# Letting a list scheduler choose VectorE or GpSimd, and DMA or TensorE, in an attention stage that runs beside a dense expert layer

## The chip, the cores and the metric

One core of a Trainium2 chip. The metric is the device time of one execution, in microseconds (us). Engine names are those of the profile: PE (TensorE matmul), PEld (its weight loads), DVE (VectorE), ACT (ScalarE), POOL (GpSimd), SP (SyncE, the queue from which the DMAs are issued).

## What is computed

Three layers follow one another; q, k and v have shape (4, 8, 576, 64).

```python
scores = scale * np.matmul(q, k.transpose(0, 1, 3, 2))     # plus a decay, causal mask
attn = np.exp(scores - max); attn = attn / (np.sum(attn) + 1e-09)
x = np.matmul(attn, v)                                      # (2304, 512)
for e in range(4):                                          # dense expert layer
    out += p[:, e:e + 1] * (np.maximum(x @ w1[e], 0.0) @ w2[e])
logits = out @ phi                                          # soft mixture: 8 experts x 4 slots
d = softmax over tokens; slot_out = experts(d.T @ out); y = softmax over slots @ slot_out
```

## The kernel before

Values are kept as two fp16 parts, a high part (the rounded value) and a low part (what rounding left), and each product is taken as high*high + high*low + low*high, so nearly every operand is made in two steps: high (ACT or POOL), then low (DVE).

**Attention.** A unit is 128 query rows of one batch with its 8 heads (18 units); a group is 1, 2 or 4 heads of a unit (76 groups). A group goes through: scores on PE (`g_scores`, L1077, two PSUM buffers `s`), row maximum on DVE (`g_max`, L1098), its product with the scale of q on POOL (`g_bias`, L1105), exp on ACT (`g_exp`, L1118), which frees the `s` buffer, the high part of the probabilities on POOL (`g_hi`, L943 by the helper `scaled`), the low part on DVE (`g_lo`, L1135), a transposition of both parts (`transposed`; by DMA at L854, or for the first groups on PE at L868 with copies out of PSUM at L873 and L875), and the product with v (`g_pv`, L1166). Two buffers hold probabilities, three hold high and low parts, five hold transposed ones. The finished unit is normalized (`fin_a`), split (`fin_h` on POOL, `fin_l` on DVE L1196) and transposed. q, k and v are scaled, split (low parts at L1018, L956, L979) and q and k transposed in the same way.

**Expert 0 beside it.** The first expert of the dense layer (`e0_l1` L526, `e0_l2` L547) takes a unit as soon as it is transposed, and fills PE between the groups. Experts 1 to 3 follow (L711 and L587): for blocks of rows their first layer is done as a fast matrix multiplication with 7 products of halves instead of 8, for which sums of x parts (`x_sums`, L631) and of weight blocks (`part` with `sub`, L475, low parts L481) are made on DVE. The last stage is the soft mixture.

**What sets the order.** `Sched` is a list scheduler that runs when the program is built. Every piece of work is a task with an engine, a cost in us, a key (its priority), the tasks it needs, and a condition on buffers. Whenever an engine is free in the scheduler's own account, the ready task of lowest key is emitted to it. On the chip each engine then runs its instructions in that order, whatever the real times. In the kernel before, only high parts of q, k, v and weights may go to either of two engines (`HI`), and every transposition has a fixed way: PE for the first few (`PE_P`, `PE_X`, `PE_Q`, `PE_K`), DMA for all others.

Of the kernel before, what the change touches and what calls it, by code (L numbers as in the profile page):

```python
# [30 lines left out]
W_COST = {"Act": 0.62, "DVE": 0.65}  # L31
X_COST = {"Act": 0.74, "DVE": 0.88}
# [6 lines left out]
PE_K = (0, 1, 2)  # L39
K_W1, K_W2, K_PB = -6, 1, 2.0  # L40
# [94 lines left out]
class Sched:  # L135
# [4 lines left out]
    DMA_HEAD, DMA_TAIL = 1.4, 1.6  # L140

# [46 lines left out]
    def run(self, done):  # L188
        while not done():
            started = False  # L190
            for e in self.engines:
# [3 lines left out]
                for x in self.ready[e]:  # L195
                    if (best is None or x.key < best.key) and (x.can is None or x.can()):
                        best = x
# [7 lines left out]
                if e == "DMA":  # L205
                    end = max(self.t + self.DMA_HEAD, self.free[e] + self.DMA_HEAD) + best.dur
                    self.free[e] = end - self.DMA_HEAD
                    end += self.DMA_TAIL
                else:
                    end = self.t + best.dur  # L210
                    self.free[e] = end
# [21 lines left out]
def moe_attention_kernel(ctx: ExitStack, tc: tile.TileContext, q, k, v, f, probs, w1, w2, phi, s1, s2, out):  # L233
# [145 lines left out]
    later = sc.later  # L379

# [34 lines left out]
    def w_steps(e, ti, pages):  # L415
# [50 lines left out]
        def lo(g):  # L466
            nc.vector.scalar_tensor_tensor(
                out=lo_[:, g * per:(g + 1) * per, :], in0=raw[g], scalar=am[:, 7:8],
                in1=hi_[:, g * per:(g + 1) * per, :], op0=ALU.mult, op1=ALU.subtract)
        def part(c, ps):  # L470
# [3 lines left out]
            def sub(out, a, b):  # L474
                return lambda: nc.vector.tensor_tensor(out=out, in0=a, in1=b, op=ALU.subtract)  # L475
# [4 lines left out]
            def lo_of(b, o):  # L480
# [6 lines left out]
                    ("DVE", sub(b11, b12, b11), (1,)), ("Act", hi_of(b22, 2), ()), ("DVE", lo_of(b21, 1), (2,)),  # L487
                    ("Act", hi_of(b11, 4), (3,)), ("DVE", lo_of(b22, 2), (4,)), ("DVE", sub(b12, b22, b12), (3,)),
                    ("DVE", sub(b22, b22, b11), (7, 8)), ("DVE", sub(b21, b21, b22), (5, 9)),
# [10 lines left out]
        X = [(lambda eng="Act", g=g: hi(g, eng), lambda g=g: lo(g)) for g in range(4)]  # L500
# [114 lines left out]
    def x_sums(p, tmp):  # L615
# [14 lines left out]
        def op(o, x, y, f, *deps):  # L630
            return ("DVE", lambda: nc.vector.tensor_tensor(out=at_(o), in0=at_(x), in1=at_(y), op=f), deps)  # L631
# [32 lines left out]
    def steps(key, todo, cost, deps):  # L664

        out = []
        for eng, fn, ds in todo:
            out.append(sc.task(eng, cost[eng], key, fn, [out[d] for d in ds] if ds else deps))
        return out

    def halves_tasks(e, w1_t, w2_t, s_t, tmps, between=lambda j: [], used_up=None):
# [24 lines left out]
        def quad(p, m, h_t):  # L696
# [26 lines left out]
            def add(o, x, n, deps, last=True):  # L723
# [4 lines left out]
                return T("DVE", 0.47, -30, go, deps)  # L728

            def split(i, c, y, t):  # L730
                h_, l_ = (z[:, y] for z in hT2[i])
                t = T("Act", 0.41, -30, lambda: nc.scalar.activation(out=h_, in_=tmp[:, c], func=AF.Relu), [t])  # L732
                t = T("DVE", 0.47, -30, lambda: nc.vector.scalar_tensor_tensor(  # L733
# [9 lines left out]
            t0 = T("Act", 0.37, -30, copy, [mul(1, a11, 0)] + mem[m % 2])  # L743
# [13 lines left out]
        def tile_l2(j, t, hs):  # L757
# [15 lines left out]
            return T("DVE", 0.66, -30, out, [y])  # L773
# [75 lines left out]
    def transposed(key, deps, dst, src, r, nw, done, can, way):  # L849

        m = r.stop - r.start
        if way == "DMA":
            def go():
                nc.sync.dma_start_transpose(out=dst(), in_=src())  # L854
                if done:
                    later(done)
            return sc.join([sc.task("DMA", 0.112 * nw * m / 128 + 0.38, key, go, deps, can)])
        cell, left, copies = {}, [], []
        t = None
        for w0 in range(0, nw, 8):  # L860
# [1165 lines left out]
```

## Time and profile before

| | |
|---|---|
| median of 3 runs | 1016.6 us (1015.73 to 1016.62) |
| the profiled execution | 1015.85 us, span in the trace 1014.1 us |
| PE busy | 924.8 us (91%) |
| DVE busy | 685.6 us (68%) |
| ACT busy | 384.3 us (38%) |
| POOL busy | 173.4 us (17%) |
| mean granted clock of PE | 0.972 |

Busy shares are means over stages with different limits: attention with expert 0 runs to about 390 us, experts 1 to 3 to about 950 us, the soft mixture to the end. The trace shows one execution; the sum of the prediction is made against its 1015.85 us, of which 1.75 us lie outside the span.

### The profile page before, as it was taken

The page shows a single profiled execution, that of the slowest core. Times are in us where ns is not written, and L with a number is a line of the kernel's source. Part 1 is how long each engine was busy: PE and PEld are TensorE (multiplying, and loading weights), DVE is VectorE, ACT ScalarE, POOL GpSimd, SP SyncE. Part 2 cuts the span into 40 slices and gives each one's busy share as a digit, 9 for nine tenths or more (in the row PEclk, how much of TensorE's full clock was granted, in tenths as well). Part 3 has the DMA queues.
Part 4 walks back from the last instruction along what each step waited for, and adds up shares of the span by engine and source line. Part 5 has one row for each costly group of instructions (what it writes and reads, how often), then busy time and mean ns, then how long its engine had stood idle before and what let it go on. Part 6 is the DMA issues. An engine that isn't in the chain of part 4 may idle for free.

```text
span 1014.1 us, 20126 instructions
## 1 busy us (share of the span) xinstructions
PE 924.8 (91%) x8165; PEld 568.3 (56%) x8165; DVE 685.6 (68%) x1408; ACT 384.3 (38%) x843; POOL 173.4 (17%) x227
## 2 busy tenths in 40 slices
PE   4478888989988998999999999999999999999994
PEld 3467676777776765446454554545455465555431
DVE  7998998896897789979467692816765283323313
ACT  7656555555654347335024440302422031112122
POOL 1755645464353300000000000000000000000000
PEclk9597999999999999999999999999999999999998
DMA  9468999999999822013201331000113028222695
GB/s 268 105 151 180 191 188 192 194 189 200 199 183 205 152 65 81 22 42 126 83 1 42 118 130 43 1 1 1 45 52 125 1 72 290 98 67 84 210 358 187
DMA packets 274413, 125.29 MB, mean 124 GB/s; under 512 B 246384, under 2 KB 246384, under 8 KB 274320
## 3 DMA queue, kind: packets, MB, share of 16 engines
q1 hardware_dynamic: 274272, 123.93, 49.5%
q8 instruction: 64, 1.05, 0.4%
q14 instruction: 29, 0.24, 0.1%
q10 hardware_dynamic: 48, 0.07, 0.0%
HBM read 73.58 MB, written 4.72 MB: 77 GB/s over the span
## 4 chain that ended last, share of the span: by engine, by line
PE 56%; DVE 7%; issue 2%; ACT 2%; DMA 1%; POOL 1%; DVEq 0%; ACTq 0%; POOLq 0%
PE pso L587 27%; PE q L711 18%; PE psh L569 3%; DVE arena L725 2%; DVE arena L631 2%; PE fh L1920 1%; PE fo L1937 1%; DVE arena L733 1%; DMA arena<-arena 1%; PE psh L526 1%; PE lg L1709 1%; PE sl L1734 1%; PE pt L1699 1%; DVE arena L481 1%; DVE arena L1135 1%
## 5 line engine op out<-in xcount | busy, mean ns | idle before, releaser
L587 PE MATMUL pso<-arena 128*128 128x512 f16 x1296 | 284.8, 379 | 1.0 <-DVE arena L733 0.9
L711 PE MATMUL q<-arena 128*128 128x384 f16 x1344 | 221.9, 326 | 2.3 <-DVE arena L725 1.4
L587 PEld LDWEIGHTS <-arena 128*128 128x128 f16 x1296 | 125.8, 98 | 153.2 <-issue 4.1
L711 PEld LDWEIGHTS <-arena 128*128 128x128 f16 x1344 | 131.2, 98 | 90.9 <-issue 3.6
L1118 ACT ACTIVATE arena<-s,mx,qs 128x320 f32<-128x320 f32 (+4 forms) x144 | 91.8, 646 | 120.4 <-POOL mx L1105 119.7
L725 DVE TENSOR_TENSOR arena<-arena,q 128x384 f32<-128x384 f32 x224 | 117.0, 548 | 18.4 <-PE q L711 16.2
L593 DVE SCALAR_TENSOR_TENSOR arena<-pso,pw,arena 128x512 f32<-128x512 f32 x54 | 40.4, 749 | 122.9 <-PE pso L587 122.8
L732 ACT ACTIVATE arena<-arena 128x384 f16<-128x384 f32 x128 | 65.8, 521 | 121.8 <-DVE arena L725 121.6
L526 PE MATMUL psh<-arena 128*128 128x128 f16 x1728 | 106.5, 224 | 4.4 <-DMA arena<-arena 1.8
L526 PEld LDWEIGHTS <-arena 128*128 128x128 f16 x1728 | 102.0, 101 | 5.3 <-issue 2.7
L547 PE MATMUL pso<-arena 128*128 128x512 f16 x432 | 99.5, 380 | 1.5 <-ACT arena L536 0.8
L1077 PE MATMUL s<-arena 128*128 128x128 f16 (+1 forms) x928 | 69.8, 219 | 31.0 <-ACT arena L1118 26.9
L1135 DVE SCALAR_TENSOR_TENSOR arena<-arena 128x512 f16<-128x512 f32 (+4 forms) x148 | 77.9, 566 | 20.2 <-POOL arena L943 20.2
L1077 PEld LDWEIGHTS <-arena 128*128 128x128 f16 x928 | 61.5, 102 | 35.7 <-issue 31.4
L733 DVE SCALAR_TENSOR_TENSOR arena<-arena 128x384 f16<-128x384 f32 x128 | 69.5, 553 | 14.3 <-ACT arena L732 9.3
L943 POOL TENSOR_SCALAR arena<-arena 128x576 f16<-128x576 f32 (+4 forms) x76 | 64.6, 850 | 56.4 <-ACT arena L1118 26.1
L1098 DVE TENSOR_REDUCE mx<-s 128x1 f32<-128x576 f32 (+4 forms) x76 | 63.6, 845 | 3.6 <-PE s L1077 3.6
L547 PEld LDWEIGHTS <-arena 128*128 128x128 f16 x432 | 40.1, 98 | 46.2 <-DVE arena L538 1.7
L1601 POOL TENSOR_SCALAR_AFFINE_SELECT arena<-arena 128x32 f32<-128x32 f32 x3 | 0.6, 216 | 379.5 <-PE q L711 379.4
L1166 PE MATMUL pv<-arena 128*128 128x64 f16 (+1 forms) x1312 | 51.7, 196 | 12.3 <-DMA arena<-arena 8.1
L1105 POOL TENSOR_SCALAR mx<-mx,qs 128x2 f32<-128x2 f32 (+2 forms) x76 | 43.8, 576 | 90.1 <-DVE mx L1098 73.6
L1166 PEld LDWEIGHTS <-arena 128*128 128x128 f16 (+1 forms) x1312 | 46.1, 101 | 19.8 <-DMA arena<-arena 10.7
(204 smaller groups left out, 966.0 us busy)
## 6 DMA issues: line engine op xcount, KB each, us to landing
arena<-in_moe_w_dram SPq DMA_DIRECT2D x58, 512.0 KB, 4.1
arena<-in_moe_w_dram SPq DMA_DIRECT2D x69, 256.0 KB, 5.1
arena<-in_moe_w_dram SPq DMA_DIRECT2D x9, 768.0 KB, 8.7
arena<-in_k_dram SPq DMA_DIRECT2D x16, 256.0 KB, 3.6
arena<-in_q_dram SPq DMA_DIRECT2D x16, 256.0 KB, 3.7
arena<-in_v_dram SPq DMA_DIRECT2D x16, 256.0 KB, 3.9
out_dram<-arena SPq DMA_DIRECT2D x16, 256.0 KB, 2.7
arena<-in_moe_w_dram SPq DMA_DIRECT2D x3, 1024.0 KB, 6.1
```

The lines of the kernel that those rows point to most:

```text
L526: nc.tensor.matmul(out=ps[:, m, :], lhsT=wt["w1" + a, 0][:, kk, ms], rhs=xT[j][:, b + kk, ts], start=(n == 0), stop=(n == 3 * KD - 1))
L547: nc.tensor.matmul(out=ops[u], lhsT=a[:, m, ts], rhs=wt["w2" + b, 0][:, m, :], start=(m == 0 and z == 0), stop=(m == KF - 1 and z == 2))
L587: nc.tensor.matmul(out=ps, lhsT=a[:, m, ts], rhs=wt["w2" + b, e][:, m, :], start=(m == 0 and z == 0), stop=(m == KF - 1 and z == 2))
L711: nc.tensor.matmul(out=ps[n], lhsT=wS[e][o][:, y, k, ms], rhs=x[z][:, k], start=(i == 0), stop=(i == 5))
L725: nc.vector.tensor_tensor(out=tmp[:, o], in0=tmp[:, x], in1=ps[n], op=ALU.add)
L732: t = T("Act", 0.41, -30, lambda: nc.scalar.activation(out=h_, in_=tmp[:, c], func=AF.Relu), [t])
L733: t = T("DVE", 0.47, -30, lambda: nc.vector.scalar_tensor_tensor(out=l_, in0=tmp[:, c], scalar=0.0, in1=h_, op0=ALU.max, op1=ALU.subtract) ...
L943: nc.gpsimd.tensor_scalar(out=out, in0=x, scalar1=scale, scalar2=0.0, op0=ALU.mult, op1=ALU.add)
L1077: nc.tensor.matmul(out=o, lhsT=qT[u][:, 2 * h + w, :], rhs=kT[kk][:, 2 * h + w, k0:k0 + n_], start=(w == 0), stop=(w == 1 and mask is None))
L1118: nc.scalar.activation(out=P[:, x], in_=sv[:, x // hb, x % hb], func=AF.Exp, scale=qs[u][:, 4:5], bias=mxs[n][:, 4 + x:5 + x], accum_out=s ...
L1135: nc.vector.scalar_tensor_tensor(out=t[:, :, d0:d0 + n_], in0=P[:, :, s0:s0 + n_], scalar=P_MUL, in1=t[:, :, s0:s0 + n_], op0=ALU.mult, op ...
L1166: nc.tensor.matmul(out=pv[u][r, h, :], lhsT=pt[:, w, r], rhs=rhs, start=(z == 0), stop=(z == len(mm) - 1))
```

## The change

- The scheduler gets costs per engine, and a rule (`soonest`): a task that may go to two engines is left for the other one if that one, with what is queued there ahead, would be done over `SLACK` sooner.
- Low parts of probabilities, q, k, v, x and expert 0's weights, and the sums for experts 1 to 3 (`x_sums`, `sub`) may go to DVE or POOL. On POOL a low part with a scale takes two instructions (scale in place, then subtract).
- exp adds ln 4096 to its bias, so its result is already scaled; the high part of the probabilities then may go to POOL or ACT, and the low part is a plain subtraction. The division by the sum takes the factor out again.
- `g_bias` moves from POOL to ACT.
- Every transposition after the first few goes to DMA, or to PE if the DMA queue is more than `T_WAIT` behind in the scheduler's account and a PSUM buffer is there; on PE it is 8 windows at a time, with a copy by DVE or ACT.
- The scheduler's costs are changed nearly everywhere, most of them upwards.

```diff
+T_WAIT = 1.0
+    def soonest(self, x, e):
+        for o in x.eng:
+            if o != e:
+                before = sum(y.dur[o] for y in self.ready[o] if y.key < x.key and len(y.eng) == 1)
+                if max(self.free[o], self.t) + before + x.dur[o] + self.SLACK < self.t + x.dur[e]:
+                    return False
+        return True
...
+    LO = ("DVE", "Pool")
+    def low(eng, out, x, scale, hi_):
+        if eng == "DVE":
+            nc.vector.scalar_tensor_tensor(out=out, in0=x, scalar=scale, in1=hi_, op0=ALU.mult, op1=ALU.subtract)
+        else:
+            nc.gpsimd.tensor_scalar(out=x, in0=x, scalar1=scale, scalar2=0.0, op0=ALU.mult, op1=ALU.add)
+            nc.gpsimd.tensor_tensor(out=out, in0=x, in1=hi_, op=ALU.subtract)
...
+        def rule(x, e):
+            return e == "DMA" or (m_can() and sc.free["DMA"] > sc.t + T_WAIT)
+        engs = ("DMA", "PE") if way == "any" else (way,)
+        sc.task(engs, {"DMA": 0.17 * nw * m / 128 + 0.05, "PE": pe_t(chunks[0][1] * m)}, key, go, deps,
+                can if way != "PE" else lambda: m_can() and (can is None or can()), rule if way == "any" else None)
...
-        nc.gpsimd.tensor_scalar(out=mx[:, 4:4 + nh], in0=mx[:, 0:nh], scalar1=qs[u][:, 4:5], scalar2=None,
-                                op0=ALU.mult)
+        nc.scalar.activation(out=mx[:, 4:4 + nh], in_=mx[:, 0:nh], func=AF.Copy, scale=qs[u][:, 4:5],
+                             bias=math.log(P_MUL))
...
-            nc.vector.scalar_tensor_tensor(out=t[:, :, d0:d0 + n_], in0=P[:, :, s0:s0 + n_], scalar=P_MUL,
-                                           in1=t[:, :, s0:s0 + n_], op0=ALU.mult, op1=ALU.subtract)
+            by[eng].tensor_tensor(out=t[:, :, d0:d0 + n_], in0=P[:, :, s0:s0 + n_], in1=t[:, :, s0:s0 + n_],
+                                  op=ALU.subtract)
...
-                t = T(P_HI, 0.1 + nh * nco * 1.0e-3, n + 0.3, lambda eng, n=n: g_hi(n, eng), [t_exp[n]], lambda: hl_r.free)
-                t = T("DVE", 0.14 + nh * nco / 960, n + 0.4, lambda n=n: g_lo(n), [t])
+                t = T(HI, hi_t(nh * nco), n + 0.3, lambda eng, n=n: g_hi(n, eng), [t_exp[n]], lambda: hl_r.free)
+                t = T(LO, lo_t(nh * nco, 1 + (i > 0)), n + 0.4, lambda eng, n=n: g_lo(n, eng), [t])
...
-                                "PE" if n < PE_P else "DMA")]
+                                "PE" if n < PE_P else "any")]
```

What the scheduler makes of it, counted over the whole program: 76 biases go from POOL to ACT; of the 148 low parts of probabilities 78 go to POOL (26,496 of 51,200 columns) and 70 stay on DVE; of the 66 low parts of q, k, v and expert 0's weights 28 go to POOL; 6 of 18 `fin_l`, 22 of 42 sums for x and 23 of 24 for weights go to POOL. ACT takes 45 high parts of probabilities and x that POOL had. 23 DMA transpositions go to PE (262 of 1,352 windows of 128 columns, and 16 of 64), whose transposing matmuls rise from 224 to 502, and their copies on DVE from 10 to 34, on ACT from 10 to 27.

Three places show it. First, SP's queue, from its first half-height transposition of k on (`128x16x64`); L854 and L920 are the transpositions, L988 and L1037 loads of q. Before:

```order
L854 DMA_TRANSPOSE arena<-arena 128x16x64
L988 DMA arena<-in_q_dram 128x8x64
L854 DMA_TRANSPOSE arena<-arena 128x9x128
L854 DMA_TRANSPOSE arena<-arena 128x16x128
L854 DMA_TRANSPOSE arena<-arena 128x9x128
L854 DMA_TRANSPOSE arena<-arena 128x16x128
L854 DMA_TRANSPOSE arena<-arena 128x9x128 x2
L854 DMA_TRANSPOSE arena<-arena 128x16x128 x2
L988 DMA arena<-in_q_dram 128x8x64
L854 DMA_TRANSPOSE arena<-arena 128x8x128 x2
```

Now:

```order
L920 DMA_TRANSPOSE arena<-arena 128x16x64
L1037 DMA arena<-in_q_dram 128x8x64
L920 DMA_TRANSPOSE arena<-arena 128x9x128 x2
L920 DMA_TRANSPOSE arena<-arena 128x16x128 x2
L920 DMA_TRANSPOSE arena<-arena 128x9x128
L1037 DMA arena<-in_q_dram 128x8x64
L920 DMA_TRANSPOSE arena<-arena 128x16x128 x2
L1037 DMA arena<-in_q_dram 128x8x64
L920 DMA_TRANSPOSE arena<-arena 128x8x128
```

One of four 9-window transpositions and one of two 8-window ones are gone from the queue and are done on PE, and the loads of q stand earlier.

Second, ACT in the unit whose groups are 2 heads of 448 columns; L1118 and L1166 are exp, L1153 the new bias, L992 high parts, L588 and L554 an eviction of expert 0. Before:

```order
L1118 ACTIVATE arena,sums<-s,mx,qs 128x448 x2
L554 ACTIVATE arena<-pso,pw 128x512
L1118 ACTIVATE arena,sums<-s,mx,qs 128x448 x4
L995 ACTIVATE arena,qs<-arena 128x512
L904 ACTIVATE arena,kvs<-arena 128x512
L875 ACTIVATE arena<-tp 128x8x128
L1118 ACTIVATE arena,sums<-s,mx,qs 128x448 x2
```

Now:

```order
L1153 ACTIVATE mx<-mx,qs 128x2
L1166 ACTIVATE arena,sums<-s,mx,qs 128x448 x2
L1153 ACTIVATE mx<-mx,qs 128x2
L1166 ACTIVATE arena,sums<-s,mx,qs 128x448 x2
L588 ACTIVATE arena<-pso,pw 128x512
L992 ACTIVATE arena<-arena 128x512
L1153 ACTIVATE mx<-mx,qs 128x2
L1166 ACTIVATE arena,sums<-s,mx,qs 128x448 x2
L1153 ACTIVATE mx<-mx,qs 128x2
L1044 ACTIVATE arena,qs<-arena 128x512
L1166 ACTIVATE arena,sums<-s,mx,qs 128x448 x2
```

Each exp has its bias just ahead of it on the same engine, and a high part stands between two groups.

Third, the end of attention. Before, DVE makes the sums of x (L631), of the weights (L475) and, among them, the low part of the last unit (L1196):

```order
L631 TENSOR_TENSOR arena<-arena 128x768 x6
L1188 TENSOR_TENSOR arena<-pv,sums 128x512
L631 TENSOR_TENSOR arena<-arena 128x768 x3
L538 SCALAR_TENSOR_TENSOR arena<-psh,arena 128x4x128
L631 TENSOR_TENSOR arena<-arena 128x768 x3
L538 SCALAR_TENSOR_TENSOR arena<-psh,arena 128x4x128
L631 TENSOR_TENSOR arena<-arena 128x768
L1196 TENSOR_TENSOR arena<-arena 128x512
```

Now POOL ends its work on attention (L1183) and takes sums of x (L665) and of weights (L509):

```order
L1183 TENSOR_TENSOR arena<-arena 128x512
L1183 TENSOR_TENSOR arena<-arena 128x64
L665 TENSOR_TENSOR arena<-arena 128x768 x5
L509 TENSOR_TENSOR arena<-arena 128x512 x8
L665 TENSOR_TENSOR arena<-arena 128x768 x17
L509 TENSOR_TENSOR arena<-arena 128x512 x15
```

On DVE the last unit's low part now directly follows its normalization, ahead of all but one sum.

## Rows read from the trace of the kernel before

**Rows 1.** The page's slices: busy tenths in 40 equal slices of the span.

```profile
PE   4478888989988998999999999999999999999994
...
PEclk9597999999999999999999999999999999999998
DMA  9468999999999822013201331000113028222695
```

**Rows 2.** Busy time by stage, the whole span.

```profile
core 0: us, PE busy (x) PEld busy (x) DVE busy (x) ACT busy (x) POOL busy (x), PEclk, DMA share, GB/s
0.00:20.00 20.00, 7.41 (x78) 5.98 (x79) 13.33 (x45) 15.98 (x30) 4.30 (x14) 1.00 0.94 256
20.00:80.00 60.00, 36.92 (x463) 31.57 (x461) 56.22 (x109) 37.95 (x91) 32.96 (x31) 0.74 0.64 152
80.00:340.00 260.00, 228.14 (x3568) 185.36 (x3568) 223.32 (x491) 142.41 (x367) 123.52 (x160) 0.97 1.03 192
340.00:390.00 50.00, 46.60 (x621) 34.58 (x620) 39.74 (x64) 25.53 (x46) 9.82 (x14) 1.00 0.42 98
390.00:490.00 100.00, 96.15 (x525) 51.16 (x526) 91.76 (x156) 41.30 (x69) 0.00 (x0) 1.00 0.21 69
490.00:1000.00 510.00, 505.37 (x2906) 258.37 (x2905) 255.76 (x539) 116.57 (x236) 2.84 (x9) 1.00 0.25 88
```

**Rows 3.** What PE waited for, 0 to 340 us: total us, times, longest.

```profile
PE s L1077 <- ACT arena L1118: 26.3, 19, 3.9
PE pv L1166 <- DMA arena<-arena: 8.1, 8, 2.6
...
PE tp L868 <- DVE arena L1135: 4.1, 2, 3.7
```

**Rows 4.** Longest waits of all engines, 0 to 350 us.

```profile
ACT arena L1118 <- POOL mx L1105: 115.8, 52, 5.5
POOL mx L1105 <- DVE mx L1098: 72.8, 39, 5.4
```

**Rows 5.** Groups of instructions on DVE: the page's, then by shape, 0 to 350 us.

```profile
L1135 DVE SCALAR_TENSOR_TENSOR arena<-arena 128x512 f16<-128x512 f32 (+4 forms) x148 | 77.9, 566 | 20.2 <-POOL arena L943 20.2
...
L979 DVE SCALAR_TENSOR_TENSOR arena<-arena,bsc 128x512 f16<-128x512 f32 x20 | 17.2, 880 | 0.0
...
L873 DVE COPY arena<-tp 128x1024 f16<-128x1024 f16 x9 | 6.0, 678 | 0.0
```

**Rows 6.** Groups of instructions on POOL: the page's, then by shape.

```profile
L1105 POOL TENSOR_SCALAR mx<-mx,qs 128x2 f32<-128x2 f32 (+2 forms) x76 | 43.8, 576 | 90.1 <-DVE mx L1098 73.6
...
L943 POOL TENSOR_SCALAR arena<-arena 128x576 f16<-128x576 f32 x30 | 22.2, 739 | 22.0 <-ACT arena L1118 13.5 <-DMA arena<-arena 7.5
```

**Rows 7.** Line L467 (low part, 1024 columns), 0 to 340, then 390 to 500 us.

```profile
L467 DVE SCALAR_TENSOR_TENSOR arena<-arena,wm x8: 1274/2090/2133, 27.3 to 60.6; 128x1024 f16<-128x1024 f32 x8
...
L467 DVE SCALAR_TENSOR_TENSOR arena<-arena,wm x8: 1274/1276/1279, 398.9 to 474.2; 128x1024 f16<-128x1024 f32 x8
```

**Rows 8.** ACT: a 2-column ACTIVATE in the timeline; groups by shape.

```profile
5.57 0.20 ACT L1487 ACTIVATE wu<-ones 128x2 f32<-128x2 f32 x1
...
L941 ACT ACTIVATE arena<-arena,bsc 128x512 f16<-128x512 f32 x10 | 7.0, 718 | 0.5 <-PE pv L1166 0.3
L875 ACT ACTIVATE arena<-tp 128x1024 f16<-128x1024 f16 x7 | 7.2, 1022 | 5.7 <-PE tp L868 5.7
```

**Rows 9.** PE: 48 matmuls and the next start; transpositions, 0 to 350 us.

```profile
353.57 2.84 PE L526 MATMUL psh<-arena 128*128 128x128 f16 x48
356.25 0.57 PE L1166 MATMUL pv<-arena 128*128 128x64 f16 x14
...
L868 PE MATMUL tp<-ident_h,arena 128*128 128x128 f16 x136 | 14.3, 263 | 11.3 <-DVE arena L1135 4.1 <-POOL arena L943 2.1 <-DVE arena L1018 1.7
```

**Rows 10.** The timeline around the end of attention: start, us, what.

```profile
360.78 5.73 DVE L631 TENSOR_TENSOR arena<-arena 128x768 f32<-128x768 f16 x6
...
378.26 5.53 PE L526 MATMUL psh<-arena 128*128 128x128 f16 x96 [1.81 <-DMA arena<-arena]
...
393.67 7.16 PE L711 MATMUL q<-arena 128*128 128x384 f16 x43 [0.91 <-DVE arena L481]
```

More of the change, by code (lines that the diff above doesn't have):

```diff
@@ L123, in __init__ @@
         self.pick = False
+        self.rule = None
         self.end = None
@@ L195, in run @@
                 for x in self.ready[e]:
-                    if (best is None or x.key < best.key) and (x.can is None or x.can()):
+                    if ((best is None or x.key < best.key) and (x.can is None or x.can())
+                            and (x.rule is None or x.rule(x, e))):
                         best = x
@@ L209, in run @@
                 else:
[L210 removed]
+                    end = self.t + best.dur[e]
                     self.free[e] = end
@@ L464, in hi, with lo @@
                                      scale=am[:, 7:8])
[L466 to L469, printed above, removed]
+        def lo(g, eng="DVE"):
+            low(eng, lo_[:, g * per:(g + 1) * per, :], raw[g], am[:, 7:8], hi_[:, g * per:(g + 1) * per, :])
         def part(c, ps):
@@ L499, in w_steps @@
         A = [lambda g=g: size(g) for g in range(4)] + [scale_a, scale_b, scale_c]
-        X = [(lambda eng="Act", g=g: hi(g, eng), lambda g=g: lo(g)) for g in range(4)]
+        X = [(lambda eng="Act", g=g: hi(g, eng), lambda eng="DVE", g=g: lo(g, eng)) for g in range(4)]
         return L, A, X
@@ L772, in tile_l2 @@
             beside()
-            return T("DVE", 0.66, -30, out, [y])
+            return T("DVE", 0.75, -30, out, [y])
         end_s, end = [], []
@@ L884, in transposed, with end, tr, cp @@
-        return sc.join(copies)
+        over = sc.handle()
+        chunks = [(w0, min(8, nw - w0)) for w0 in range(0, nw, 8)]
+        left = list(chunks)
+        def end():
+            if done:
+                done()
+            sc.close(over)
+        def tr(w0, n):
+            m_take((key, w0))
+            d = dst()
+            ps = ps_m.tile([128, 8, m], F16, tag="m", name="tp")
+            for w in range(n):
+                nc.tensor.transpose(ps[:, w, :], src()[:, (w0 + w) * 128:(w0 + w + 1) * 128], ident_h[r, r])
+            def cp(eng):
+                if eng == "DVE":
+                    nc.vector.tensor_copy(d[:, w0:w0 + n, :], ps[:, 0:n, :])
+                else:
+                    nc.scalar.activation(out=d[:, w0:w0 + n, :], in_=ps[:, 0:n, :], func=AF.Copy)
+                def given():
+                    m_give((key, w0))
+                    left.remove((w0, n))
+                    if not left:
+                        end()
+                later(given)
+            sc.task(("DVE", "Act"), {"DVE": 0.1 + n * m * 0.58e-3, "Act": 0.18 + n * m * 0.83e-3}, key, cp, [sc.now])
@@ new lines, in go, with pe_t @@
+        def go(eng):
+            if eng == "DMA":
+                nc.sync.dma_start_transpose(out=dst(), in_=src())
+                later(end)
+                return
+            tr(*chunks[0])
+            for c in chunks[1:]:
+                sc.task("PE", pe_t(c[1] * m), key, lambda c=c: tr(*c), [sc.now], m_can)
+        def pe_t(cols):
+            return 0.15 + cols * 0.45e-3
+        def rule(x, e):
+            return e == "DMA" or (m_can() and sc.free["DMA"] > sc.t + T_WAIT)
+        engs = ("DMA", "PE") if way == "any" else (way,)
```

169 lines of the change are left out of this document (76 added, 93 removed).

## The prediction, as put on record before the run

> **What bounds the kernel now.** I read the slices first. PE is busy at nine tenths almost everywhere except in the first tenth of the span, and its clock falls there alone [rows 1]. Cut by stage [rows 2], PE idles 12.6 us in 0 to 20 us, 23.1 in 20 to 80, 31.9 in 80 to 340, 3.4 in 340 to 390, 3.9 in 390 to 490, and 4.6 in the 510 us after that. So the time is PE's work plus 75 us of holes before 490 us, nearly all in attention; what the change does after 490 us can't matter. In attention DVE is the other full engine: 56.2 of 60 us and 223.3 of 260 us, the DMA engines are at 1.03 of their capacity in 80 to 340 us, while POOL has 123.5 and ACT 142.4 of 260 us [rows 2]. Now the waits. The largest of PE's own is for exp, which has to free a score buffer (26.3 us, 19 times), then for transposed probabilities from DMA (8.1 us) [rows 3]. Behind the exp, ACT waits 115.8 us for the bias on POOL, and POOL 72.8 us for the maximum on DVE [rows 4]: the chain is maximum, bias, exp, and DVE's queue is the longest part of it. PE runs its instructions in order, so when a score waits, the expert-0 matmuls behind it wait too.
>
> **The change, part by part.**
>
> *Transpositions on PE.* 278 more matmuls. In the same shape 48 take 2.68 us start to start [rows 9], 56 ns each: 278 x 56 ns = **+15.5 us** of PE work. Least 0 (they fall into holes), most 29 us (105 ns each, from 14.3 us for 136 [rows 9], partly at the low clock). I take 15.5, as most run in 80 to 340 us, where the clock is 0.97. They also bring waits: before, PE stood 11.3 us ahead of 17 blocks of 8 [rows 9], 0.66 us each; 278 are 35 blocks, so 0 to 23 us. Queued behind are scores, products with v and expert 0. I take **+2.5**, near the low end: a block is given to PE only when its low part is done in the scheduler's account and DMA is late.
>
> *The chain to exp.* A bias on POOL takes 576 ns [rows 6], one on ACT about 0.20 [rows 8]: 76 x 0.38 = 29 us less in the chain, at the price of 15 us of ACT time. DVE's queue in front of the maximum gets shorter: 52% of the 77.9 us of low parts goes [rows 5], 40 us; 28 low parts at 0.88 [rows 5] are 25; 6 `fin_l` some 4; the copies for PE add 24 at up to 0.68 [rows 5], some 14. Net 55 of the 293 us that DVE is busy in 0 to 340 us: 86% becomes 70%. Since 29 us plus a share of the 72.8 leave a chain of 115.8 us of waits [rows 4], I let 60% of PE's 26.3 us go: **-16**, between 0 and -26.
>
> *What POOL takes.* No row has a two-input instruction on POOL. One input of 576 columns takes 739 ns, 1.28 ns a column [rows 6]; the least for two inputs is that, the most I allow twice, 2.57. At the upper end 26,496 columns are 68 us and 28 low parts of 512 columns, each with its scaling, 0.66 + 1.31 us, 55 us. Less 43.8 us of biases [rows 6] and 45 high parts at about 0.75, 34 us: POOL's 161 us in 0 to 340 us become 206, 61%. It has room, so I put no term; if its cover (idle POOL) were gone, a low part of 576 columns would come 0.8 us later, and a probability buffer with it. The Trainium skill (GPSIMD Engine Reference, section 3.1) gives 4497 ns for a two-input add of 2048 columns, 2.2 ns a column; by that estimate POOL comes to some 190 us and the sum stays the same.
>
> *What ACT takes.* 45 high parts at 0.72 or a little over [rows 8], 35 us; 17 copies at 1.02 [rows 8], 17; 15 of biases. With 196 us before (16.0 + 38.0 + 142.4 [rows 2]) some 263 of 340 us, 77%, as it filled its waits for the bias. No term, but a rival.
>
> *DMA.* 20% of the transposed windows leave a queue at 1.03 [rows 2], and the loads of q behind them start earlier: of PE's 8.1 us for transposed probabilities [rows 3] I let **-5** go, between 0 and -8.
>
> *The start.* In 20 to 80 us DVE is full (94%) while PE idles 23.1 us [rows 2]. The order puts about 7 low parts, one weight low part of 2.09 us [rows 7] and two halves of probabilities of that stretch on POOL, some 9 us. I take **-5**, between 0 and -9.
>
> *The end of attention.* DVE's sums run back to back, six in 5.73 us, PE stands 1.81 us for the last transposition, which waits for a low part behind those sums, and 0.91 us for a weight's low part [rows 10]. Now POOL has half of the sums. Of 7.3 us of holes in 340 to 490 us [rows 2] I take **-4**, between 0 and -7; the sums are a serial chain, slower on POOL, hence no more.
>
> Other scheduler costs, the early place of loads and the moved factor of 4096 have no price of their own: they only set the order, which is in the terms above.
>
> Sum: 15.5 + 2.5 - 16 - 5 - 5 - 4 = **-12 us**, 1015.85 to 1003.85 for the profiled execution; the median of the runs lies 0.75 above it, so **1004.6 us**.
>
> **Rivals.**
>
> *Holes nearly vanish.* With every recovery at its upper end (26 + 8 + 9 + 7) and only the transpositions' 15.5 against it, -35: 982. For it: all other engines come under 80%. Against: PE, at 228 of 260 us, would have to reach 94% or more with matmuls of different lengths. I take 980 to 995, chance 0.14, most likely 988.
>
> *VectorE and GpSimd hold each other.* The same low part of 1024 columns takes 1.28 us when POOL is idle and 2.09 us in the median when it works [rows 7]; so part of what leaves DVE comes back as longer instructions. If the 99 low parts left on DVE meet POOL busy 61% of the time and lose 0.4 us, half of what that row lost, per meeting, 24 of the 55 us are back, DVE stays at 77%; exp's recovery halves to -8, and -4 is left: 1012, between 1010 and 1018. Chance 0.13. The Trainium skill (SBUF — State Buffer, "Who interferes with whom") says that a DVE instruction with two SBUF inputs and a POOL instruction that reads SBUF lock each other out for the whole instruction; by that rule the new two-input POOL work holds DVE longer than the old. The trace agrees so far, by the 1.28 and 2.09 us.
>
> *PE's queue stops at the transpositions* (slower). A DMA transposition waits in SP's queue, one on PE holds everything behind it. If a block waits as those before did, 35 x 0.66 = 23 us come [rows 9], and half of the recoveries (15 of 30) are lost since PE is late for the rest: 15.5 + 23 - 15 = +23, 1040; at half that wait +12, 1029. It decides from some 14 us of such waits on, if the other recoveries stand (2.5 are in the sum). Against it: the rule takes PE only where DMA is late. Chance 0.14.
>
> *ACT's queue.* Exp may now stand behind a high part or a copy. If a quarter of these 52 us falls on the chain, 13 us are added where 16 go in the forecast: +17, 1022. For it: 77% with six kinds of work in one queue. Chance 0.09.
>
> That the change doesn't do what it says I leave out: the order shows the moved instructions.
>
> **How the numbers follow.** Forecast 0.50 (996 to 1012), holes vanish 0.14, engines hold each other 0.13, PE's queue 0.14, ACT's queue 0.09. The range 985 to 1023 leaves out half of the second case below, and above most of the fourth and a third of the fifth, some 0.2. A difference of 0.2% (2 us) is about what a measurement of this kernel can tell from none. Faster than 1014.6: the first two and a small part of the third, 0.66; within 1014.6 to 1018.6: 0.09; slower: 0.25. The likeliest case has its own range, 996 to 1012.
>
> **What would show it.** The PE row by stage: holes in 80 to 340 us should shrink from 31.9 to some 12 while PE's busy time before 390 us grows by about 15. The wait of scores for exp should be about 10 us, that of ACT for a bias gone. DVE should be near 70% in attention, ACT near 77%, POOL near 60%. If transposing matmuls head PE's waits with over 14 us, the third rival holds; if scores wait for exp over 26 us with ACT busy, the fourth; if DVE's low parts of probabilities take well over their mean of 0.57 us [rows 5], the second. The stage after 490 us must keep its length; if it doesn't, I have missed something.

## The result and the profile after

The changed kernel takes 1007.25 us (median of 4 runs, 1005.39 to 1007.75), beside 1016.6 us for the kernel before on the same chip: 0.9907 of it, 95% interval 0.9888 to 0.9927. A fourth run of the kernel before took 1939.89 us and is left out. The forecast was 1004.6 us. The profiled execution took 1005.39 us, its span is 1003.5 us, 10.6 us less than before. PE is busy for 933.7 us (before 924.8), so its holes fell by 19.5 us and its work rose by 8.9.

The windows by stage of the changed kernel, with the columns of [rows 2]:

```profile
20.00:80.00 60.00, 40.63 (x551) 35.23 (x548) 54.24 (x107) 46.81 (x113) 45.61 (x42) 0.77 0.53 126
80.00:340.00 260.00, 250.26 (x4121) 207.01 (x4119) 208.25 (x420) 204.14 (x504) 171.96 (x192) 1.00 0.91 173
340.00:390.00 50.00, 42.73 (x365) 26.82 (x363) 46.01 (x52) 29.84 (x47) 30.14 (x18) 0.97 0.17 59
390.00:490.00 100.00, 94.92 (x489) 48.87 (x489) 75.27 (x117) 30.21 (x52) 24.26 (x13) 0.97 0.20 69
490.00:1000.00 510.00, 498.99 (x2869) 254.75 (x2867) 258.40 (x525) 119.99 (x243) 26.73 (x24) 1.00 0.27 94
```

PE's holes in 80 to 340 us fell from 31.9 to 9.7 us. In 340 to 490 us they rose from 7.3 to 12.4. PE's waits in 0 to 340 us answer [rows 3]:

```profile
PE mp L419 <- DVE arena L906: 7.7, 1, 7.7
...
PE s L1125 <- ACT arena L1166: 5.6, 3, 3.3
PE tp L902 <- DVE arena L1008: 3.8, 2, 2.8
PE tp L902 <- DVE arena L1243: 2.9, 4, 1.4
```

Scores wait 5.6 us for exp instead of 26.3, and the products with v wait 0.7 us for DMA instead of 8.1. The wait of 7.7 us is new: at 28.9 to 36.6 us a small product stands until DVE has copied transposed windows out of PSUM (L906), and DVE's queue has three low parts of weights ahead of that copy, 7.18 us together. So a transposition on PE also costs a place in DVE's queue. In the waits of all engines, what answers [rows 4] is one line:

```profile
ACT mx L1153 <- DVE mx L1146: 37.8, 34, 5.3
```

The groups of instructions, 0 to 350 us (the POOL row by shape), answer [rows 5], [rows 8] and [rows 9]:

```profile
L1183 DVE TENSOR_TENSOR arena<-arena 128x512 f16<-128x512 f32 (+4 forms) x70 | 42.6, 649 | 10.9 <-POOL arena L994 6.6 <-ACT arena L992 4.2
L1153 ACT ACTIVATE mx<-mx,qs 128x2 f32<-128x2 f32 (+2 forms) x76 | 21.9, 293 | 38.1 <-DVE mx L1146 37.8
L1183 POOL TENSOR_TENSOR arena<-arena 128x512 f16<-128x512 f32 x32 | 39.1, 1222 | 15.4 <-ACT arena L992 13.9
L902 PE MATMUL tp<-ident_h,arena 128*128 128x128 f16 (+1 forms) x430 | 36.0, 230 | 15.5 <-DVE arena L1008 3.8 <-DVE arena L1243 2.9 <-POOL arena L994 2.1
```

The end of attention, PE's timeline, answers [rows 10]:

```profile
342.44 0.57 PE L1214 MATMUL pv<-arena 128*128 128x64 f16 x14
...
366.62 6.61 PE L581 MATMUL pso<-arena 128*128 128x512 f16 x22 [4.69 <-DVE arena L572]
373.06 2.11 PE L746 MATMUL q<-arena 128*128 128x384 f16 x12
375.32 0.46 PE L419 MATMUL mp<-ident,wm 128*128 128x128 f32 x2
375.62 11.95 PE L746 MATMUL q<-arena 128*128 128x384 f16 x72
391.34 4.58 PE L746 MATMUL q<-arena 128*128 128x384 f16 x18 [3.77 <-DVE arena L760]
```

Three marks follow from such rows: the end of the last product with v (343.0 us here), the end of expert 0 on PE (373.2, before 388.97) and the start of expert 1. Expert 0 ends 15.7 us earlier, but from there to the second block of expert 1's first layer (443.48, before 453.59) it takes 70.3 us instead of 64.6. So 5.7 of the 15.7 us are lost just behind.

### The profile page after: what moved, and what is told of

Its sections match the earlier page's. It is cut to its first block, busy times and chain, and to the rows that moved or that the text cites. A ratio compares the mean times of both kernels' runs of the same rounds, so it can differ in the third digit from the quotient of the medians.

```text
span 1003.5 us, 20699 instructions
## 1 busy us (share of the span) xinstructions
PE 933.7 (93%) x8443; PEld 577.8 (58%) x8443; DVE 655.4 (65%) x1260; ACT 445.3 (44%) x983; POOL 306.9 (31%) x304
## 4 chain that ended last, share of the span: by engine, by line
PE 76%; DVE 12%; issue 4%; POOL 3%; ACT 3%; DMA 1%; SPq 0%; DVEq 0%; POOLq 0%; ACTq 0%
PE pso L621 28%; PE q L746 20%; PE pso L581 6%; PE psh L560 5%; PE psh L603 3%; PE s L1125 3%; PE pv L1214 2%; DVE arena L411 2%; PE fh L1973 1%; PE fo L1990 1%; DVE mx L1146 1%; POOL arena L1183 1%; DVE arena L768 1%; DVE arena L515 1%; ACT arena L1166 1%
## 5 line engine op out<-in xcount | busy, mean ns | idle before, releaser
L746 PE MATMUL q<-arena 128*128 128x384 f16 x1344 | 224.6, 329 | 7.5 <-DVE arena L760 7.5
L760 DVE TENSOR_TENSOR arena<-arena,q 128x384 f32<-128x384 f32 x224 | 117.5, 551 | 29.2 <-PE q L746 20.8
L509 POOL TENSOR_TENSOR arena<-arena 128x512 f32<-128x512 f32 x23 | 37.2, 1617 | 287.0 <-DVE arena L515 281.5
L560 PE MATMUL psh<-arena 128*128 128x128 f16 x1728 | 102.4, 220 | 1.6 <-DVE qs L399 1.2
L1166 ACT ACTIVATE arena<-s,mx,qs 128x320 f32<-128x320 f32 (+4 forms) x144 | 91.7, 644 | 2.4
L768 DVE SCALAR_TENSOR_TENSOR arena<-arena 128x384 f16<-128x384 f32 x128 | 81.4, 649 | 5.5 <-ACT arena L767 1.8
L1125 PE MATMUL s<-arena 128*128 128x128 f16 (+1 forms) x928 | 68.2, 217 | 5.9 <-ACT arena L1166 5.6
L1183 POOL TENSOR_TENSOR arena<-arena 128x512 f16<-128x512 f32 (+3 forms) x78 | 68.5, 898 | 15.9 <-ACT arena L992 13.9
L774 ACT ACTIVATE arena<-q 128x384 f32<-128x384 f32 x32 | 15.6, 486 | 116.3 <-PE q L746 116.3
L994 POOL TENSOR_SCALAR arena<-arena 128x576 f16<-128x576 f32 (+4 forms) x49 | 38.8, 795 | 62.1 <-ACT arena L1166 61.6
L665 POOL TENSOR_TENSOR arena<-arena 128x768 f32<-128x768 f32 (+2 forms) x22 | 42.1, 1924 | 32.8 <-DVE arena L665 17.0
```

The source lines that it names most:

```text
L560: nc.tensor.matmul(out=ps[:, m, :], lhsT=wt["w1" + a, 0][:, kk, ms], rhs=xT[j][:, b + kk, ts], start=(n == 0), stop=(n == 3 * KD - 1))
L665: return (LO, lambda eng: by[eng].tensor_tensor(out=at_(o), in0=at_(x), in1=at_(y), op=f), deps)
L746: nc.tensor.matmul(out=ps[n], lhsT=wS[e][o][:, y, k, ms], rhs=x[z][:, k], start=(i == 0), stop=(i == 5))
L760: nc.vector.tensor_tensor(out=tmp[:, o], in0=tmp[:, x], in1=ps[n], op=ALU.add)
L768: t = T("DVE", 0.55, -30, lambda: nc.vector.scalar_tensor_tensor(out=l_, in0=tmp[:, c], scalar=0.0, in1=h_, op0=ALU.max, op1=ALU.subtract) ...
L1125: nc.tensor.matmul(out=o, lhsT=qT[u][:, 2 * h + w, :], rhs=kT[kk][:, 2 * h + w, k0:k0 + n_], start=(w == 0), stop=(w == 1 and mask is None))
```

## The experiments

All run against the kernel before; ratios carry their 95% interval. The runs used several chips, on which the kernel before took 1015.98 to 1016.94 us in the median. Each is the changed kernel with the edit shown.

### Who takes back 5 us after attention

**e_both_dve**: the sums for x and the weight differences on DVE only.

```diff
-            return (LO, lambda eng: by[eng].tensor_tensor(out=at_(o), in0=at_(x), in1=at_(y), op=f), deps)
+            return ("DVE", lambda: by["DVE"].tensor_tensor(out=at_(o), in0=at_(x), in1=at_(y), op=f), deps)
...
-                    (LO, sub(b11, b12, b11), (1,)), ...
+                    ("DVE", sub(b11, b12, b11), (1,)), ...
```

> The changed kernel, with the sums of x and the differences of weight blocks for experts 1 to 3 made by VectorE alone, as before the change. Theory (VectorE and GpSimd hold each other): between expert 0's end on PE and the second block of expert 1 the changed kernel takes 70.3 us against 64.6 before; with GpSimd idle there this falls to 64 to 66 us, low parts at 0.55 us each instead of up to 1.99, and the time to 1001 to 1003 us. Rival (VectorE needs the relief): VectorE gets 23 x 0.68 + 22 x 0.95 = 36 us of work back, stays the bound there, and the time is 1007 to 1011 us.

**e_sums_dve** puts only the first of the two edits in, **e_subs_dve** only the second.

> The changed kernel with only the sums of x back on VectorE; the differences of weight blocks stay where the scheduler puts them. If the long GpSimd sums (1.64 us alone) are what holds VectorE's low parts of expert 1 (up to 1.99 us for 0.55), most of the 5.6 us comes back here: 1002 to 1004 us. If the weight differences are, 1006 to 1008 us.

> The changed kernel with only the differences of weight blocks back on VectorE; the sums of x stay where the scheduler puts them. If these 23 instructions on GpSimd hold the weights' low parts (up to 2.13 us for 0.74) and with them PE's 4.7 us wait for expert 0's low part, 1002 to 1004 us; if the sums of x do the harm, 1005 to 1008 us.

Measured: 999.24 us (0.9824, 0.9809 to 0.984) for both, 999.57 (0.9828, 0.9812 to 0.9845) for the sums, 1005.52 (0.9885, 0.9867 to 0.9903) for the weight differences. The low parts of experts 1 to 3 on DVE, by line, columns: minimum, median and maximum in ns; first the changed kernel, then with both on DVE:

```profile
L768 DVE SCALAR_TENSOR_TENSOR arena<-arena x128: 546/553/1994, 379.2 to 830.9; 128x384 f16<-128x384 f32 x128
```

```profile
L768 DVE SCALAR_TENSOR_TENSOR arena<-arena x128: 546/551/559, 381.5 to 824.3; 128x384 f16<-128x384 f32 x128
```

e_both_dve and e_sums_dve came out below the ranges of their theories (1001 to 1003 and 1002 to 1004), e_subs_dve in the range for the sums of x as the cause. PE stood 4.69 and 3.77 us in the rows above; this is what POOL and DVE did in these two waits of the changed kernel:

```profile
361.89 3.52 POOL L509 TENSOR_TENSOR arena<-arena 128x512 f32<-128x512 f32 x2 [0.69 <-DVE arena L515]
362.54 3.42 DVE L515 SCALAR_TENSOR_TENSOR arena<-arena,wm 128x512 f16<-128x512 f32 x2
365.88 0.68 DVE L572 SCALAR_TENSOR_TENSOR arena<-psh,arena 128x512 f16<-128x512 f32 x1
...
386.32 8.58 POOL L665 TENSOR_TENSOR arena<-arena 128x768 f16<-128x768 f32 x4 [0.41 <-ACT arena L668]
386.92 3.91 DVE L768 SCALAR_TENSOR_TENSOR arena<-arena 128x384 f16<-128x384 f32 x2
390.75 1.00 DVE L760 TENSOR_TENSOR arena<-arena,q 128x384 f32<-128x384 f32 x2
```

What follows: on POOL a two-input sum of 768 columns takes 1.92 us in the mean (the page: 42.1 us for 22), and a two-input low part on DVE that meets one takes up to 1994 ns instead of 551. The instructions that PE waits for are not longer themselves (L572 takes 693 ns at most, L760 558; each has one input in PSUM). They stand in DVE's queue behind low parts that are: in the first wait behind two low parts of weights that meet weight differences on POOL, in the second behind two low parts that meet sums of x. Taking the sums back is worth 8 us; for the weight differences alone the two intervals overlap, so nothing is shown. DVE had gained no time from giving this work away: with all of it back, some 36 us by the sum in the expectation, DVE is busy for 656.2 us of the whole span instead of 655.4. The Trainium skill (SBUF — State Buffer, "Who interferes with whom") says that a DVE instruction with two SBUF inputs and a POOL instruction that reads SBUF contend for a port pair under an exclusive lock; the trace agrees, 1994 ns beside 559.

### What the transpositions on PE are worth

**e_no_pe_tr**: the changed kernel with all later transpositions by DMA again.

```diff
-                                "PE" if n < PE_P else "any")]
+                                "PE" if n < PE_P else "DMA")]
```

(the same for q, k and x).

> The changed kernel with every transposition after the first few by DMA again; the rest stays. By the prediction's terms (15.5 us of PE work and 2.5 us of waits against 5 us of waits for DMA) this would be some 13 us faster: 994 us. Rival (PE had the room, DMA had not): the DMA engines go back over 1.0 of their capacity in 80 to 340 us, products with v wait 8 us or more for them, score buffers stay taken, and the time is 1008 to 1015 us.

Measured 1027.91 us (1.0109, 1.0091 to 1.0128): 20.7 us slower than the changed kernel and slower than the kernel before, though biases, high and low parts all keep their new freedom, and above both ranges. Its window 80 to 340 us, and two of its waits in 0 to 350 us:

```profile
80.00:340.00 260.00, 232.68 (x3622) 192.74 (x3620) 192.61 (x398) 189.32 (x477) 142.66 (x156) 0.93 1.00 188
```

```profile
POOL arena L994 <- DMA arena<-arena: 24.6, 7, 10.2
PE s L1125 <- DMA arena<-arena: 10.2, 3, 5.9
```

DVE, ACT and POOL all have room; the DMA engines are at 1.00. The last product with v, first in the kernel before, then in this one:

```profile
365.34 0.57 PE L1166 MATMUL pv<-arena 128*128 128x64 f16 x14
```

```profile
363.95 0.57 PE L1214 MATMUL pv<-arena 128*128 128x64 f16 x14
```

Attention ends 1.4 us earlier than in the kernel before, and 21.5 later than in the changed kernel. What makes it slower than the kernel before comes behind attention: from expert 1's first product (385.88 us) to the end of the span it takes 638.7 us, the kernel before 623.3. The sums on POOL, which cost 8 us above, are still there; whether they alone explain it was not run.

**e_only_pe_tr**: of the choices, that between DMA and PE alone (biases and high parts on POOL, low parts and sums on DVE, with the new costs). **e_only_costs**: that one with the edit above too, so that only the scheduler's costs and the factor of 4096 are new.

> Of the change only the choice between DMA and PE for transpositions and the scheduler's new costs: biases and high parts on GpSimd, low parts and sums on VectorE, as before the change (the factor 4096 stays in the bias). Theory after e_no_pe_tr (the transpositions on PE carry the gain, some 20 us): 999 to 1006 us. Rival (each part is needed, since VectorE full holds PE's transpositions): 1009 to 1018 us.

> The kernel before with the scheduler's new costs and the factor of 4096 in exp, but without any choice of engine: all later transpositions by DMA, biases and high parts on POOL, low parts and sums on DVE. It differs from the run with the choice between DMA and PE alone (1010.1) by the transpositions only. Theory (what pays is that PE takes work from a full DMA queue; costs only set the order): within 6 us of the kernel before, 1012 to 1022, DMA share about 1.0 in 80 to 340 us and scores again waiting over 20 us for exp. Rival (the corrected costs make the better order, and the transpositions on PE bring nothing): 1006 to 1012, as with the choice.

Measured 1010.08 us (0.9925, 0.9903 to 0.9948) and 1017.64 us (1.0017, 1.0004 to 1.003). The first came out as its rival said, the second as its theory. The costs alone gain nothing; the transpositions on PE alone are worth 7.6 us by the medians and 9 by the ratios, since the two ran on different chips. Attention's last product ends at 364.2 us without them and at 353.3 with them. In all three kernels that transpose by DMA it ends at 364 to 366 us, with the DMA engines at 1.00 to 1.04 of 80 to 340 us, whatever the other engines do: **the DMA queue set the end of attention**.

**e_hi_twait0**: the opposite direction, on the best kernel below, more transpositions on PE.

```diff
-T_WAIT = 1.0
+T_WAIT = 0.0
```

> The best run so far (high parts on POOL, sums on DVE; 994.0) with the threshold T_WAIT at 0, so that about 170 more windows are transposed on PE (17 fewer DMA transpositions). At 56 ns each they cost PE some 10 us. Theory (the first transpositions on PE were worth more than they cost because DMA was at its limit; now DMA is at 0.94 of 80 to 340 us, and little is left to gain): 996 to 1004, DMA share near 0.85, PE's busy time before 390 us up by 8 to 10. Rival (DMA still sets the pace): 985 to 992.

Measured 1010.48 us (0.9944, 0.9924 to 0.9964), 16.5 us slower than with 1.0, above both ranges. DMA fell from 0.94 to 0.81. The transposing matmuls, with 1.0 and with 0.0:

```profile
L902 PE MATMUL tp<-ident_h,arena 128*128 128x128 f16 (+1 forms) x454 | 37.8, 230 | 14.1 <-DVE arena L1008 5.3 <-DVE arena L1183 2.3 <-POOL arena L994 2.1
```

```profile
L902 PE MATMUL tp<-ident_h,arena 128*128 128x128 f16 (+1 forms) x625 | 51.9, 228 | 14.5 <-DVE arena L1008 2.7 <-DVE arena L1183 2.5 <-POOL arena L994 2.1
```

171 more took 14.1 us, 82 ns each where I had 56, and PE's whole busy time rose from 930.5 to 948.3 us, while its holes stayed (61.7 and 60.2). The first product of expert 1 starts at 388.6 us instead of 371.1. With DMA below its limit the loss is PE's own work.

### Bias, low parts, high parts

**e_both_bias_pool**, on e_both_dve: the biases on POOL again.

```diff
-        nc.scalar.activation(out=mx[:, 4:4 + nh], in_=mx[:, 0:nh], func=AF.Copy, scale=qs[u][:, 4:5],
-                             bias=math.log(P_MUL))
+        nc.gpsimd.tensor_scalar(out=mx[:, 4:4 + nh], in0=mx[:, 0:nh], scalar1=qs[u][:, 4:5],
+                                scalar2=math.log(P_MUL), op0=ALU.mult, op1=ALU.add)
```

> The kernel of e_both_dve (999.2 us) with the biases of exp made by GpSimd again, their factor ln 4096 included. Theory (the chain to exp): GpSimd now has 172 of 260 us of other work in 80 to 340 us, a bias stands behind low parts of up to 1.6 us, ACT's wait for it comes back to 60 us or more, scores wait for exp 15 to 25 us instead of 6: 1006 to 1014 us. Rival (PE has the room since the transpositions moved, the bias never mattered): 998 to 1002 us.

Measured 1006.18 us (0.9891, 0.9871 to 0.991): the biases on ACT are worth 6.9 us here. Scores wait 11.1 us for exp and ACT 45.3 for a bias, both less than the theory said.

**e_both_lo_dve**, on e_both_dve: all low parts on DVE (the first edit). **e_both_hi_pool**, on e_both_dve: high parts of probabilities and x on POOL only (the second). **e_bias_tr**: both edits, so that only transpositions and biases are chosen anew.

```diff
-    LO = ("DVE", "Pool")
+    LO = ("DVE",)
```

```diff
-                t = T(HI, hi_t(nh * nco), n + 0.3, lambda eng, n=n: g_hi(n, eng), [t_exp[n]], lambda: hl_r.free)
+                t = T(("Pool",), hi_t(nh * nco), n + 0.3, lambda eng, n=n: g_hi(n, eng), [t_exp[n]], lambda: hl_r.free)
...
-            t = T(HI, {"Pool": 0.75, "Act": 0.65}, n + 0.7, lambda eng, u=u: fin_h(u, eng),
+            t = T(("Pool",), {"Pool": 0.75, "Act": 0.65}, n + 0.7, lambda eng, u=u: fin_h(u, eng),
```

> The kernel of e_both_dve with every low part of attention on VectorE. Theory (VectorE was the full engine): it gets some 55 us back, is at 85% or more in 80 to 340 us, the maximum comes later: 1004 to 1010 us. Rival (the two engines hold each other, so that GpSimd's low parts cost VectorE as much as they take): VectorE's two-input instructions shorten by a third, 998 to 1001 us.

> The kernel of e_both_dve with the high parts of probabilities and x on GpSimd alone, as before the change. Theory: GpSimd gets 35 us back and the scheduler gives it fewer low parts; the probabilities wait for it, 1001 to 1006 us. Rival (ACT at 79% is the engine in the way of exp): relief for ACT, 996 to 999 us.

> Only two parts of the change, transpositions by DMA or PE and the biases on ACT, with high parts on POOL and low parts and sums on DVE. Theory (the two gains add: 1010.1 with the transpositions alone, less the 5 to 7 us that the biases or the high parts were worth in the other runs; low parts on POOL bring nothing in any arrangement): 993 to 1000, like the best run (994.0), with DVE at about 230 of 260 us. Rival (once ACT is relieved DVE is the next limit, and the low parts on POOL are then needed): 1001 to 1007, scores waiting over 15 us for exp.

Measured 1000.45 us (0.9844, 0.9814 to 0.9873), **993.97 us** (0.9771, 0.9755 to 0.9787; the best kernel of all) and 1007.33 us (0.9911, 0.9895 to 0.9928). So the two freedoms stand in for each other. With high parts free to go to ACT, low parts on POOL gain nothing (999.24 and 1000.45); with high parts on POOL they gain 13 us. My expectation that they bring nothing in any arrangement is wrong. e_both_hi_pool is faster than either of its ranges allowed. What the biases are worth depends on the rest too: from e_only_pe_tr (1010.08) to e_bias_tr (1007.33) it is 2.7 us, and the intervals overlap.

For e_both_lo_dve the time is the rival's and DVE's load the theory's. In 80 to 340 us, first e_both_dve, then e_both_lo_dve:

```profile
80.00:340.00 260.00, 250.28 (x4113) 206.79 (x4111) 208.79 (x425) 204.94 (x506) 172.03 (x193) 1.00 0.92 174
```

```profile
80.00:340.00 260.00, 249.50 (x4011) 204.56 (x4009) 230.31 (x519) 195.88 (x491) 77.63 (x83) 0.99 0.97 175
```

POOL's 94 us of additional work in this stretch takes 21.5 us off DVE. By an estimate from the counts and means by shape of both kernels, the work given to POOL is worth 56 us of DVE time (copies for PE taken off), and what stayed on DVE took 23 us longer in sum. So DVE and POOL do hold each other in attention. But attention ends at 343.9 and 343.7 us, so DVE's load, even at 89%, did not set its end in these two kernels.

### Where the difference sits: the handover to expert 1

Times of the profiled executions, in us, from PE's and DVE's timelines. "Parts" is the end of the last of the 14 low parts of expert 1's first weights (L515; L481 before) on DVE.

| kernel | last product with v | parts | expert 0 ends | expert 1 starts | span |
|---|---|---|---|---|---|
| before | 365.9 | 394.3 | 389.0 | 390.8 | 1014.1 |
| only costs | 364.2 | 392.3 | 381.3 | 392.2 | 1014.5 |
| only PE/DMA choice | 353.3 | 383.8 | 371.7 | 383.7 | 1007.5 |
| e_bias_tr | 351.7 | 382.0 | 374.4 | 381.9 | 1005.5 |
| the change | 343.0 | 373.5 | 373.2 | 373.1 | 1003.5 |
| e_both_dve | 343.9 | 373.1 | 367.6 | 373.0 | 997.1 |
| e_both_lo_dve | 343.7 | 372.8 | 365.0 | 372.7 | 996.6 |
| e_both_hi_pool | 339.4 | 368.6 | 371.3 | 371.1 | 992.2 |

From the end of attention to the last weight part it takes 28 to 31 us in each: DVE's sums for x, then the weight parts, one after another. In all but the kernel before, expert 1 starts when these are there or when expert 0 is done, whichever is later, to within 0.5 us. (The kernel before starts it 3.5 us ahead of the last part, and PE then waits 0.91 us for a part [rows 10].) From this start to the end of the span it takes 621 to 624 us in every kernel of the table except the change, where it takes 630 with the sums on POOL; so among the others the start of expert 1 is where the difference sits. In e_both_lo_dve expert 0 is done early and PE stands:

```profile
359.62 5.34 PE L581 MATMUL pso<-arena 128*128 128x512 f16 x24
372.09 0.77 PE L419 MATMUL mp<-ident,wm 128*128 128x128 f32 x2 [7.13 <-DVE wm L474]
372.65 29.85 PE L746 MATMUL q<-arena 128*128 128x384 f16 x168
```

In e_both_hi_pool attention ends 4.3 us earlier, so the parts do, and expert 0 still fills PE until then:

```profile
365.94 5.34 PE L581 MATMUL pso<-arena 128*128 128x512 f16 x24
371.12 27.46 PE L746 MATMUL q<-arena 128*128 128x384 f16 x168
```

**e_lo_dve_mp6** asks whether the small product `mp`, which waits for DVE's queue ahead of expert 1, is the cause or only first in line.

```diff
-        t = sc.task("PE", 0.3, key, go, deps, m_can)
+        t = sc.task("PE", 0.3, key, go, deps, lambda: m_can() and ok())
...
+            first = pe_next[0]
+            ok = (lambda: pe_next[1] >= first + 6) if (e, ti) == (1, 1) else (lambda: True)
```

> The run with all low parts and sums on DVE (1000.45) with one thing moved: the small product on PE that makes the scale of expert 1's second weight (the line of `spread`, `mp` from `wm`) may start only after six products of expert 1, not ahead of the first. All of attention keeps its order. There PE stood 7.1 us in that product for a reduction on DVE (`wm`) that is queued behind expert 1's weight parts. Theory (this handover between expert 0 and expert 1, and not attention, holds what differs between the runs with the sums on DVE): expert 0 ends again at 365 us, expert 1's first product follows within 2 us, and the time is 993 to 997. Rival (DVE's weight parts are the limit and the small product was only the first in line): PE waits as long in expert 1's first products, 999 to 1002.

Measured 998.89 us (0.9838, 0.9823 to 0.9853), 1.6 us less than e_both_lo_dve, whose four runs spread from 998.3 to 1003.32; the intervals don't separate the two, and the result lies between the two ranges. PE's timeline:

```profile
360.44 5.34 PE L584 MATMUL pso<-arena 128*128 128x512 f16 x24
365.62 1.63 PE L749 MATMUL q<-arena 128*128 128x384 f16 x9
371.59 0.82 PE L749 MATMUL q<-arena 128*128 128x384 f16 x2 [4.34 <-ACT arena L515]
372.76 6.43 PE L749 MATMUL q<-arena 128*128 128x384 f16 x25 [0.35 <-DVE wm L475]
```

Expert 1 starts at once and stands 4.3 us after nine matmuls, for the high part of a weight block on ACT (L515 in this kernel), which itself starts only when DVE has made a difference of blocks (at 370.8 us). The rival holds: the serial parts are the limit. An earlier end of attention moves the handover (e_both_hi_pool); fewer steps between the two should as well, but that was not run.

## Why the prediction came out as it did

The time is 2.65 us above the forecast and well inside its own range of 996 to 1012. That it came so close is in part luck. The forecast had +15.5 us for PE's work and -27.5 for its holes; the profiles show +8.9 and -19.5, and the two misses cancel. Term by term:

- **Transpositions on PE, +15.5 and +2.5.** Their group grew from 15.2 us (152 matmuls in the whole program) to 36.0 (430), 20.8 us, 75 ns each, and the waits ahead of them from 11.3 to 15.5. Undersized by 7 us together. But all of PE's busy time rose by 8.9 us only: rows of matmuls overlap their neighbours, the scores' group fell from 69.8 to 68.2 us and expert 0's first layer from 106.5 to 102.4, and the granted clock in 80 to 340 us rose from 0.97 to 1.00. How much each of these is, I did not resolve.
- **The chain to exp, -16.** The wait of scores fell by 20.7 us, a little more than I took. ACT does wait for the maximum still, 37.8 us, but no longer for a bias. Of the cause I had only half: the biases are worth 6.9 us in one arrangement and 2.7 in another, and with the transpositions alone the wait already falls from 22.7 us (only costs) to 13.9.
- **DMA, -5 (0 to -8).** This is the step that failed. I read the DMA engines at 1.03 [rows 2] and then priced them by PE's 8.1 us of waits for DMA alone [rows 3]. A full queue shows itself at its other users as well: the high parts on POOL wait 7.5 us for DMA in [rows 6], 24.6 in e_no_pe_tr and 0.7 in the changed kernel, and in e_no_pe_tr scores wait 10.2 us for transposed operands. How these waits add up to a later end of attention was not separated. By my terms the kernel without transpositions on PE would take 1007.25 less 18, plus 5: 994 us; it takes 1027.91.
- **The start, -5.** Holes in 0 to 80 us fell from 35.7 to 33.2 us: 2.4.
- **The end of attention, -4.** Wrong in sign: the holes in 340 to 490 us rose by 5.1. I wrote that the sums are slower on POOL, but not that each of them holds DVE.
- **DVE's relief, 55 us.** The rival of VectorE and GpSimd holding each other had its mechanism right, in attention too: it took 24 of the 55 us back, and between e_both_lo_dve and e_both_dve 23 of 56 come back as longer instructions. The low parts of probabilities, which I had named as its sign, are only a small part of it: 649 ns instead of 566, 70 x 83 ns = 6 us. The price that it drew from this was wrong: scores gained 20.7 us, not 8, and a run with all low parts back on DVE is no slower.
- **POOL and ACT.** POOL is busy for 226 of 340 us, 66% (forecast 61), ACT for 265, 78% (77), DVE for 276, 81% instead of 70. A two-input low part of 512 columns on POOL takes 1222 ns, 2.39 ns a column, within my bounds of 1.28 and 2.57. The bias on ACT takes 293 ns, not 200; the row I took it from reads no scale from memory.
- The stage after 490 us kept its length: from the second block of expert 1 to the end 560.0 us beside 560.5. In 490 to 1000 us PE is busy for 499.0 us (before 505.4), but this window now reaches to 3.5 us before the end instead of 14.1.

Of the other rivals, "holes nearly vanish" did not come, but the argument against it was wrong: PE did reach 250.26 of 260 us, 96%, and e_both_hi_pool, at 994, lies in its range. "PE's queue stops at the transpositions" did not come either. Its sign, over 14 us of waits ahead of transposing matmuls, was badly set: they have 15.5 us, of which 11.3 were there before. In e_hi_twait0, with 171 more of them, it is 14.5. "ACT's queue" did not come: scores wait 5.6 us for exp with ACT at 78%.

What stays open: why high parts on POOL bring the end of attention from 343.9 to 339.4 us with low parts on both engines, and delay it from 343.7 to 351.7 with low parts on DVE. Both runs differ in the whole order of the scheduler, and no run separates order from engine load.

## What to carry to other kernels

A transfer queue at its limit must be priced by taking work off it, not by the waits that name it: it shows as waits on engines that look free. Moving two-input work from VectorE to GpSimd costs VectorE as well, so it pays only where VectorE's instructions next to it are not on the path. Behind a stage that is shortened stands the serial preparation of the next one; look at which of the two ends last at the handover before counting the whole gain.

## What was not expected of the hardware

A stall at the handover costs more than its length. The same 168 matmuls of expert 1 took 27.46 us in e_both_hi_pool, where PE came from full work, and 30.30 in e_both_dve, behind a wait of 4.86 us. There the granted clock (the last column but two) shows why. First e_both_dve, then the first 9 us of these matmuls in e_both_hi_pool:

```profile
372.42 0.77 PE L419 MATMUL mp<-ident,wm 128*128 128x128 f32 x2 [4.86 <-DVE wm L474]
372.98 30.30 PE L746 MATMUL q<-arena 128*128 128x384 f16 x168
```

```profile
362.00:372.00 10.00, 5.56 (x31) 2.48 (x28) 9.77 (x16) 7.43 (x14) 0.00 (x0) 0.98 0.15 53
372.00:382.00 10.00, 9.58 (x41) 5.30 (x42) 7.92 (x17) 5.46 (x7) 0.00 (x0) 0.67 0.00 1
382.00:403.00 21.00, 21.00 (x131) 12.57 (x129) 20.45 (x40) 8.92 (x17) 0.00 (x0) 1.00 0.08 26
```

```profile
371.00:380.00 9.00, 9.00 (x57) 5.38 (x56) 8.68 (x12) 5.19 (x7) 0.00 (x0) 1.00 0.35 112
```

In the 10 us behind the wait the clock is 0.67 of full in the mean, so for two thirds of that time it stood at the lower of its two levels, 1.2 instead of 2.4 GHz; in e_both_hi_pool it is 1.00 over the same matmuls. The 5.4 us of the handover thus cost 8.3. A longer wait need not cost more of this: behind 7.13 us in e_both_lo_dve the same matmuls took 29.85 us.

A copy of 1, 2 or 4 columns on ACT with its scale from memory took 293 ns in the mean. The Trainium skill (ScalarE: Activation LUTs, "What ACT_TABLE_LOAD costs") gives 186 ns and 0.833 ns a column with immediate operands, and some 93 more for each that is a pointer. By that an estimate for 2 columns is 188 ns without and 281 with one pointer; the trace is near both, with 0.20 us in [rows 8] and 293 ns here.
